# A dense layer with GELU, forward and backward: the first 256 rows of x loaded plainly and turned by TensorE, with changes of order in the first steps, a load moved to another queue, and a last copy made whole

## The chip, the cores and the metric

The kernel runs on one core of a Trainium2 chip. Times are device microseconds of that core, from runs of the whole program. Before the change three runs gave a median of 267.5 us (267.42 to 267.94). A core has five engines with queues of their own: PE (TensorE, matrix products; its weight loads are PEld), DVE (VectorE), ACT (ScalarE), POOL (GpSimd) and SP (SyncE, here only for issuing transfers). Each engine runs its instructions in program order and waits on semaphores for the others.

## The reference, cut to what matters

```python
B, S, D, F = 1, 2048, 448, 1792          # all bf16

def _fwd_reference(x, w1, b1, w2, b2):
    h = jnp.einsum("bsd,df->bsf", x, w1) + b1
    h = jax.nn.gelu(h, approximate=True)
    return jnp.einsum("bsf,fd->bsd", h, w2) + b2

def reference(x, w1, b1, w2, b2, grad_out):
    out, vjp = jax.vjp(_fwd_reference, x, w1, b1, w2, b2)
    return (out, *vjp(grad_out))          # out, gx, gw1, gb1, gw2, gb2
```

With u = x w1 + b1 and h = gelu(u) this is: the output h w2 + b2; q = grad_out w2^T; gh = q times the slope of gelu at u; gx = gh w1^T; gw1 = x^T gh; gw2 = h^T grad_out; and the two bias gradients as sums over the rows of gh and grad_out.

## The kernel before, in words

The 2048 rows are four blocks of 512 (`NB`), the 1792 columns of w1 fourteen tiles of 128, taken in seven pairs a block (`NPAIR`), which makes 28 pairs. For a pair, PE computes u transposed into PSUM (`pu`: three full tiles of 128 of x's 448 columns, and a tail of 64), ACT or DVE copy it out with the bias (`copy_u`, L339 and L341), ACT makes its square, its gelu (`hT`) and a tanh, DVE the slope; PE computes q transposed (`pq`), and DVE multiplies the two into `ghT` (L397). The products of `hT` with w2 and of `ghT` with w1 transposed ("units", tiles `ps`) are PE work that is laid between the pairs' own: each unit is a bank of 128 rows by 448 columns, summed over 14 tiles in two row halves of 64, lower and upper; `side_by_side` issues the halves of two banks alternately. Where one bank is taken up with the other half, `half_product` (L253) puts a wait of PE for its own last product there.

The first 12 pairs are done one by one, with pair f = i + 2 being started in step i; the other 16 are done two by two. All of that order is written out by hand. In single step i PE takes: the first tile of u of pair f (`side_by_side(u_of(f, 0, True), ...)`), a piece of unit work `between[0]`, the second tile of u, `between[1]`, the tails, and so on. In step 1 `between[0]` is the second pair's two tiles for the two units of `uns[1]`. In the loop of double steps, `ahead` (L658) says how many of the three parts of the next pair's first tile come ahead of two units' lower halves; the rest comes between these and the upper halves, 3 in the first double step and 1 later.

At the start, all inputs are fetched by an ordered list of transfers. SP's list begins with x's first block, transposed by the transfer itself in two halves of 256 rows (L146, L149; `wide` reads 512 columns from each row, so that the tail tile's lower 64 rows hold what follows the row, against zero rows in `wt1`), then w1's columns 768 to 1024, a part of w2, grad_out's first block transposed (`load_g(0)`), w2 transposed in parts, and so on. ACT's list has w1's columns 256 to 512 and their rest (the 64 last rows of w1, `load_rest`), the load of its function table with a first activation, then w1's columns 512 to 768 and the rest of 512 to 1024. POOL clears `b1_rows` and fetches b1 into it; DVE turns that in 32 by 32 blocks (L186, L187). PE runs `NWAKE` products of ones (L184) into a bank that nobody reads, and then pair 0 (`pe_u_fulls(0)`, L238, in two halves of 256 rows, for each of the two tiles three products) and its tails (`pe_tail_zeros`, L499).

After the pairs come the weight gradients: gw1 and gw2 by products over all 2048 rows (L768, L779, L800), with the bias sums by DVE (`emit_sum`) and POOL's all-reduce over the partitions (L748, L759) beside them. `gw2_tile` makes the last one in two halves; the second half's bank is copied out by ACT and DVE, half each (L804, L806), and stored by a transfer from ACT's queue. The last lines make SP wait for the last transfers and copies.

The functions that the diff touches:

Of the kernel before, what the change touches and what calls it, by code (L numbers as in the profile page):

```python
# [10 lines left out]
ALU = mybir.AluOpType  # L11
BF16 = mybir.dt.bfloat16
# [7 lines left out]
def kernel(  # L20
# [16 lines left out]
    P = 128  # L37
# [11 lines left out]
    NSTEP = NB * NPAIR  # L49
    NSINGLE = 12  # L50
    LEAD = 2
    NWAKE = 11
    STG = 5
    ROW0 = [SB, 2 * SB, 3 * SB, 0]
    WIDE = (0, 1)
# [82 lines left out]

    AZ = tmp.tile([P, 12, SB], BF16, name="AZ", tag="AZ", bufs=1)
    ones = nc.const_aps.tensor(1.0, [P, SB], BF16)  # L140
    nc.vector.memset(wt1[DL:P, 256:768], 0.0)
    nc.gpsimd.memset(b1_rows[:], 0.0)
    nc.gpsimd.dma_start(out=b1_rows[0:NF, :], in_=b1.rearrange("(ft p) -> ft p", p=P))
    xT[0] = blk.tile([P, KF + 1, SB], BF16, name="xT", tag="xT")
    halves = [slice(0, SB // 2), slice(SB // 2, SB)]
    nc.sync.dma_start_transpose(out=xT[0][:, :, halves[0]], in_=wide(x2, ROW0[0], SB // 2, 0))  # L146
    load_w1(nc.scalar, 256, 512)
    load_rest(nc.scalar, 256, 512)
    nc.sync.dma_start_transpose(out=xT[0][:, :, halves[1]], in_=wide(x2, ROW0[0] + SB // 2, SB // 2, 0))  # L149
    warm = stg.tile([P, 1], F32, name="warm", tag="warm", bufs=1)  # L150
    behind(nc.scalar, nc.scalar.activation(out=warm[:], in_=ones[:, 0:1], func=ACT.Gelu_apprx_tanh))
    load_w1(nc.scalar, 512, 768)
    load_rest(nc.scalar, 512, 1024)
    load_w1(nc.sync, 768, 1024)
    load_w2(nc.sync, 2, 4)
    load_g(0)
# [18 lines left out]
    load_rest(nc.gpsimd, 0, 256)  # L175
    nc.gpsimd.tensor_copy(out=w2T[DL:P, 0, 0:16], in_=w2_first[0:DL, :])
    load_w2T(0, 256)
    for t0, t1 in ((0, 8), (8, NF)):
        nc.sync.dma_start_transpose(out=w1T_sb[:, t0:t1, :], in_=w1[:, t0 * P:t1 * P])
    load_g(1)  # L180

    pw = two_banks(1, "pw")
    for w in range(NWAKE):
        nc.tensor.matmul(pw[:, 0, :], lhsT=ones[:, 0:P], rhs=ones, start=True, stop=True)  # L184
    for c in range(P // 32):
        nc.vector.transpose(b1_t16[c * 32:(c + 1) * 32, :], b1_rows[:, c * 32:(c + 1) * 32])  # L186
    nc.vector.tensor_copy(out=b1T[:], in_=b1_t16[:, 0:NF])  # L187
# [44 lines left out]
    def pe_u_fulls(f):  # L232
        b, p = divmod(f, NPAIR)
        open_u(f)
        for rs in halves if f == 0 else [slice(0, SB)]:
            for a in range(2):
                for kt in range(KF):
                    nc.tensor.matmul(PU[f][a][:, rs], lhsT=w1_f[:, kt, cols(p, a)], rhs=xT[b][:, kt, rs],  # L238
                                     start=(kt == 0 and rs.start == 0), stop=False, skip_group_check=True)

# [309 lines left out]
    for i in range(1, NSINGLE):  # L550
        f = i + LEAD
        if i < 6:
            between = [(uns[1], False, tiles(i)), (uns[0], True, tiles(i)[:1]), (uns[0], True, tiles(i)[1:]), (uns[1], True, tiles(i))]
        elif i == 6:
            between = [(uns[0], True, tiles(i)), (uns[1], False, tiles(i)[:1]), (uns[1], False, tiles(i)[1:]), (uns[1], True, tiles(i))]
        else:
            if i == 7:
                ahead, later = xs, two_units((2, 3))
                slots = [(ahead, False, t) for t in range(6, NF)] + [(later, False, t) for t in range(NF)]
                slots += [(ahead, True, t) for t in range(NPAIR)] + [(later, True, t) for t in range(NF)]  # L560
                slots += [(ahead, True, t) for t in range(NPAIR, NF)]
            between = [slots[2 * c:2 * c + 2] for c in range(5)]
            del slots[0:10]
        open_u(f)
        open_q(i)
        side_by_side(u_of(f, 0, True), u_of(f, 1, True))
        fill(between[0])
        side_by_side(u_of(f, 1), u_of(f, 0))
        fill(between[1])
        pe_tail_pair(f, i, 1)  # L570
        pe_tail_pair(f, i, 0)
        fill(between[2])
        side_by_side(q_of(i, 0), q_of(i, 1))
        fill(between[3])
        side_by_side(q_of(i, 1, True), q_of(i, 0, True))
        if i < 6:
            units_side(uns[0], False, tiles(i + 1))
        elif i > 6:
            fill(between[4])
        if i > 1:  # L580
            act_tanh([i])
        if i == 6:
            evictions(2)
        copy_u(f, "aa")
        if i == NSINGLE - 1:
            evictions(2)
        act_square([f])
        if i == NSINGLE - 1:
            evictions()
        act_gelu([f])  # L590
        if i == 1:
            dve_chain("both 1", "cubic 2", "gate 1", "cubic*u 2", "slope 2", "gh 1", "slope*h 2", "cubic 3")
        elif i < NSINGLE - 1:
            dve_chain(f"both {i}", f"cubic*u {i + 1}", f"gate {i}", f"slope {i + 1}", f"gh {i}", f"slope*h {i + 1}", f"cubic {f}")
        else:
            dve_chain(f"both {i}", f"cubic*u {i + 1}", f"gate {i}", f"slope {i + 1}", f"slope*h {i + 1}", f"gh {i}",
                      f"cubic {f}", f"cubic*u {f}", f"slope {f}", f"slope*h {f}")
        if i == 6:
            evictions()
            open_two(1, 2)  # L600
            xs = open_units[-2:]
            units_side(xs, False, range(0, 6))
        if i == 9:
            nc.gpsimd.dma_start(out=g_low[0:DL, :], in_=gT[1][DL:P, 0, :])
            g_swap[1] = g_low
        if i < 8 or i % 2:
            traffic(i if i < 8 else (i + 7) // 2)
        if i >= 6:
            stores(1 if i > 7 and i % 2 else 2, f - 1)
# [23 lines left out]
    for n in range(nq):  # L633
        i = 10 + n
        k = NSINGLE + 2 * n
        ks = [k, k + 1]
        fs = [k + 2, k + 3] if k + 2 < NSTEP else []
        nxt = [k + 4, k + 5] if k + 4 < NSTEP else []
        if n == 0:
            evictions()  # L640
        act_tanh(ks)
        if n > 0:
            dve_gate(ks, evictions)
        if n == 0:
            pe_u_rows(fs)
        if fs:
            pe_tails(fs if n == 0 else fs[::-1], ks[::-1])
        for f in fs[::-1]:
            copy_u(f, "aa")
        pe_q_rows(ks, nxt)  # L650
        if n == 0:
            a_ = part_a(ks)
            nc.vector.tensor_scalar(out=a_, in0=a_, scalar1=1.0, scalar2=math.sqrt(0.5), op0=ALU.add, op1=ALU.mult)
            dve_chain(f"tanh {k + 1}", f"gate {k + 1}", f"tanh {k}", f"gh {k + 1}", f"gate {k}", f"gh {k}")
        else:
            for q in ks[::-1]:
                dve_gh(q)
        ahead = 1 if n else KF  # L658
        if nxt:
            open_u(nxt[0])  # L660
            side_by_side(u_of(nxt[0], 0, True), u_of(nxt[0], 1, True), slice(0, ahead))
            open_two(1, 2)
            uns = open_units[-2:]
            units_side(uns, False)
            side_by_side(u_of(nxt[0], 0, True), u_of(nxt[0], 1, True), slice(ahead, None))
            units_side(uns, True)
            side_by_side(u_of(nxt[1], 1), u_of(nxt[1], 0))
            side_by_side(u_of(nxt[0], 1), u_of(nxt[0], 0))
        elif fs:
            uns, held = two_units(order_a[2:4]), two_units(order_a[0:2])  # L670
            units_side(uns, False)
            units_side(held, False)
            pe_tails([], [k + 2, k + 3])
            units_side(uns, True)
        if fs:
            act_square(fs)
            act_gelu(fs)
            dve_cubic(fs)
        if i == 15:
            nc.gpsimd.dma_start(out=g_low[DL:P, :], in_=gT[3][0:DL, 0, :])  # L680
            g_swap[3] = g_low
        traffic(i)
        stores(3, k + 1)
# [45 lines left out]
    def f_at(slot):  # L729
        return (2 * FP[slot // 2] + slot % 2) * P  # L730

    sums = []
    for st_ in range(1, NS):
        sums.append(("g", st_))
# [3 lines left out]
    def emit_sum(n):  # L738
        for _ in range(n):
# [10 lines left out]
            else:  # L750
                v = acc[:].rearrange("p (ft f) -> p ft f", f=P)
                b, j = PLACE[st_]
                in0 = gh_nat[:, PLACE[0][0], :, PLACE[0][1], :] if st_ == 1 else v
                nc.vector.tensor_tensor(out=v, in0=in0, in1=gh_nat[:, b, :, j, :], op=ALU.add)  # L754
                if st_ == NS - 1:
                    gb1_w = blk.tile([P, F], BF16, name="gb1_w", tag="ghT")
                    for c in range(4):
# [37 lines left out]
    def gw2_tile(ft, halves):  # L795
        w = D // halves
        for h in range(halves):
            ps = bank_v()
            for st_ in range(NS):
                nc.tensor.matmul(ps[:, 0:w], lhsT=h_nat[ft][:, st_, :], rhs=g_nat[:, st_, h * w:(h + 1) * w],  # L800
                                 start=(st_ == 0), stop=(st_ == NS - 1))
            o = stg.tile([P, SB], BF16, name="st", tag="st")
            c = w // 2 if h == 1 else w
            done = [nc.scalar.copy(out=o[:, 0:c], in_=ps[:, 0:c])]  # L804
            if c < w:
                done.append(nc.vector.tensor_copy(out=o[:, c:w], in_=ps[:, c:w]))  # L806
            queued.append(nc.scalar.dma_start(out=out_4[ft * P:(ft + 1) * P, h * w:(h + 1) * w], in_=o[:, 0:w]))
        return done

# [10 lines left out]
            load_h(ft + 4)  # L820
        emit_sum(3)

    for what in pooled[-8:] + queued[-9:-1] + last:
        behind(nc.sync, what)


# [28 lines left out]
```

## Time and profile before

| | us |
|---|---|
| median of 3 runs | 267.5 |
| the profiled execution, whole | 267.85 |
| its span, first to last instruction | 266.1 |
| first wake-up product of PE starts | 0.77 |
| first product of pair 0 starts | 5.58 |
| PE's wait for the third pair's copies ends | 15.56 |
| first all-reduce of POOL starts | 187.86 |
| last copy's store is issued | 263.60 |

All rows of the profile come from that one profiled execution, on the clock of its span. A row of the timeline gives start, length, engine, line, operation, output and input, count, and in brackets how long the engine stood idle before it and what ended that. The lengths of products are modelled with their pipeline, so the distance between starts says more than a length. "xN" after a row are N instructions merged.

### The profile page before, as it was taken

Reading aid. Unit: us, or ns where it says so; the run is one execution under the profiler, and the core shown is the slowest. Engines: PE = TensorE matmul, PEld = TensorE weight load, DVE = VectorE, ACT = ScalarE, POOL = GpSimd, SP = SyncE. Lnnn points to the kernel's source line nnn. Section 1 sums busy time; section 2 is a strip of 40 time slices with the busy share of each in tenths; the row PEclk is TensorE's granted clock in tenths of the full one; section 3 lists DMA queues with packets and bytes.
Section 4 is the critical chain, followed back from the end, with each engine's and each line's share of the span. In section 5 each row is a group of like instructions: output and inputs, shape, how many; then the busy total and the mean of one; then the engine's idle time right before and its main releaser. Section 6 shows DMA issues by size and latency. Waiting matters only on the chain.

```text
span 266.1 us, 5210 instructions
## 1 busy us (share of the span) xinstructions
PE 261.9 (98%) x2171; PEld 167.8 (63%) x2171; DVE 175.3 (66%) x218; ACT 137.4 (52%) x164; POOL 41.5 (16%) x52
## 2 busy tenths in 40 slices
PE   8999999999999999999999999999999999999995
PEld 3456668888866565555658888864444765555554
DVE  1599999999998978769897731129999990000000
ACT  2799997887997686878759410022111111121111
POOL 1001002400302021010301120220700008900000
PEclk9999999999999999999999999999999999999999
DMA  7999999999999997364381359999311102999841
GB/s 174 243 264 187 171 225 174 286 242 188 233 204 234 211 257 178 41 172 90 115 160 44 72 121 299 352 159 281 90 40 39 49 22 55 218 216 222 203 122 35
DMA packets 111735, 44.47 MB, mean 167 GB/s; under 512 B 91040, under 2 KB 110576, under 8 KB 111712
## 3 DMA queue, kind: packets, MB, share of 16 engines
q1 hardware_dynamic: 104608, 36.14, 64.5%
q0 software_dynamic: 1856, 4.30, 6.6%
q10 hardware_dynamic: 5248, 3.71, 4.6%
q8 instruction: 17, 0.28, 0.4%
q14 instruction: 6, 0.05, 0.1%
HBM read 7.23 MB, written 14.23 MB: 81 GB/s over the span
## 4 chain that ended last, share of the span: by engine, by line
PE 95%; ACT 2%; DMA 1%; DVE 0%; issue 0%; ACTq 0%
PE ps L259 31%; PE ps_v L800 15%; PE pq L259 15%; PE pu L259 14%; PE ps_w L768 14%; PE ps_w L779 2%; PE pw L184 2%; ACT AZ L348 1%; PE pu L238 1%; ACT hT L345 1%; ACT U L339 1%; DMA out_dram<-st 1%; DVE U L341 0%; PE pu L499 0%; ACT AZ L357 0%
## 5 line engine op out<-in xcount | busy, mean ns | idle before, releaser
L259 PE MATMUL pq<-gT,w2T 64*128 64x512 bf16 x386 | 57.5, 376 | 0.0
L259 PE MATMUL ps<-w_sb,hT 64*128 64x448 bf16 x440 | 53.1, 349 | 0.1
L259 PE MATMUL ps<-w1T_sb,ghT 64*128 64x448 bf16 x448 | 51.2, 349 | 0.0
L259 PE MATMUL pu<-xT,w_f 64*128 64x512 bf16 x300 | 43.7, 376 | 0.2 <-ACT U L339 0.2
L339 ACT ACTIVATE U<-pu,b1T 128x512 bf16<-128x512 f32 x54 | 33.5, 690 | 19.3 <-PE pu L259 14.8
L800 PE MATMUL ps_v<-g_nat,h_nat 128*128 128x448 bf16 (+1 forms) x240 | 42.6, 340 | 0.0
L397 DVE SCALAR_TENSOR_TENSOR ghT<-AZ,pq 128x1024 bf16<-128x1024 bf16 x28 | 33.9, 1218 | 12.6 <-PE pq L259 12.0
L438 POOL DMA_DIRECT2D out_dram<-st x32 | 19.9, 626 | 135.8 <-DVE st L437 72.9
L259 PEld LDWEIGHTS <-ghT 64*128 64x128 bf16 x448 | 34.2, 94 | 10.0
L259 PEld LDWEIGHTS <-hT 64*128 64x128 bf16 x440 | 30.0, 94 | 14.6 <-PE ps L259 0.5
L259 PEld LDWEIGHTS <-w2T 64*128 64x128 bf16 x392 | 30.8, 94 | 10.5 <-PE pq L259 0.3
L768 PE MATMUL ps_w<-gh_nat,x_nat 128*128 128x512 bf16 (+1 forms) x192 | 36.5, 352 | 0.0
L800 PEld LDWEIGHTS <-h_nat 128*128 128x128 bf16 x240 | 23.3, 98 | 19.3 <-DMA out_dram<-st 0.3
L357 ACT ACTIVATE AZ<-AZ 128x1024 bf16<-128x1024 bf16 (+1 forms) x20 | 27.8, 1392 | 6.8 <-DVE AZ L353 6.8
L754 DVE TENSOR_TENSOR acc<-acc,gh_nat 128x1792 f32<-128x1792 f32 x14 | 30.0, 2142 | 0.5
L768 PEld LDWEIGHTS <-x_nat 128*128 128x128 bf16 x192 | 18.7, 98 | 17.9 <-issue 0.4
L806 DVE CAST st<-ps_v 128x112 bf16<-128x112 f32 x1 | 0.3, 275 | 43.1 <-DMA out_dram<-st 43.1
L348 ACT ACTIVATE AZ<-U 128x1024 bf16<-128x1024 bf16 (+1 forms) x21 | 28.2, 1342 | 0.9 <-DVE U L341 0.4
L345 ACT ACTIVATE hT<-U 128x1024 bf16<-128x1024 bf16 (+1 forms) x22 | 28.0, 1277 | 0.0
L259 PEld LDWEIGHTS <-w_f 64*128 64x128 bf16 x300 | 21.3, 94 | 10.3 <-issue 0.9
L804 ACT CAST st<-ps_v 128x448 bf16<-128x448 f32 (+2 forms) x15 | 7.5, 501 | 34.8 <-PE ps_v L800 34.8
L435 ACT CAST st<-ps 128x448 bf16<-128x448 f32 x16 | 7.8, 539 | 29.5 <-PE ps L259 27.6
(57 smaller groups left out, 197.0 us busy)
## 6 DMA issues: line engine op xcount, KB each, us to landing
hT_dram<-hT SPq DMA_DIRECT2D x28, 256.0 KB, 3.0
out_dram<-st POOLq DMA_DIRECT2D x32, 112.0 KB, 4.8
x_nat<-in_x_dram SPq DMA_DIRECT2D x1, 1792.0 KB, 10.4
g_nat<-in_grad_out_dram SPq DMA_DIRECT2D x1, 1792.0 KB, 15.7
out_dram<-st ACTq DMA_DIRECT2D x13, 112.0 KB, 3.3
out_dram<-st ACTq DMA_DIRECT2D x9, 128.0 KB, 1.7
w_f<-in_w_dram SPq DMA_DIRECT2D x5, 192.0 KB, 4.2
w_sb<-in_w_dram SPq DMA_DIRECT2D x4, 224.0 KB, 4.0
```

What stands on the lines that cost most here:

```text
L259: mm = nc.tensor.matmul(ps, lhsT=w, rhs=m, start=start, stop=stop, tile_position=(hf.start, 0), skip_group_check=True)
L339: nc.scalar.activation(out=dst, in_=PU[f][a][:], func=ACT.Identity, bias=bias)
L345: nc.scalar.activation(out=rows(hT, r), in_=part_u(r), func=ACT.Gelu_apprx_tanh)
L348: nc.scalar.activation(out=part_a(ks), in_=part_u(ks), func=ACT.Square, scale=math.sqrt(3.0 * GELU_A * GELU_C))
L357: nc.scalar.activation(out=z, in_=z, func=ACT.Tanh, scale=-1.0 / 3.0)
L397: nc.vector.scalar_tensor_tensor(out=rows(ghT, [k]), in0=part_z([k]), scalar=1.0, in1=PQ[k][:], op0=ALU.subtract if single else ALU.add, o ...
L435: nc.scalar.copy(out=st[:, 0:D], in_=self.ps)
L438: pooled.append(nc.gpsimd.dma_start(out=(out2 if self.kind == "o" else gx2)[r:r + P, :], in_=st[:, 0:D]))
L754: nc.vector.tensor_tensor(out=v, in0=in0, in1=gh_nat[:, b, :, j, :], op=ALU.add)
L768: nc.tensor.matmul(ps[:, 0:n * P], lhsT=x_nat[:, st_, kt * P:(kt + 1) * P], rhs=gh_nat[:, b, ft0:ft0 + n, j, :], start=(st_ == 0), stop=(s ...
L800: nc.tensor.matmul(ps[:, 0:w], lhsT=h_nat[ft][:, st_, :], rhs=g_nat[:, st_, h * w:(h + 1) * w], start=(st_ == 0), stop=(st_ == NS - 1))
L804: done = [nc.scalar.copy(out=o[:, 0:c], in_=ps[:, 0:c])]
```

## The change

Ten places change. At the start, rows 512 to 767 of x (the first half of the first block) are loaded untransposed into a corner of the scratch tile `AZ`, two rows on each partition; PE turns them by eight products with an identity of 128 by 128, which POOL makes, into four banks; ACT and DVE copy these into `xT[0]`. DVE clears the tail tile's lower rows of that half. There are 7 wake-up products in place of 11. w1's columns 512 to 768 are fetched by SP behind x's second half, not by ACT. The second part of w1 transposed is fetched after grad_out's second block. In `pe_u_fulls` the order of the six products of a half becomes kt outside, tile inside. In step 1 `between[0]` comes ahead of the first tile of u, and `between[1]` behind it. In the first double step `ahead` is 2. The last half of gw2 is copied by ACT alone, and SP's last waits name the last sum of DVE and that copy.

```diff
-    NWAKE = 11
+    NWAKE = 7
...
+    x_rows = AZ[:, 10:12, :].rearrange("p a s -> p (a s)")[:, 0:2 * D].rearrange("p (j d) -> p j d", j=2)
+    ident = const.tile([P, P], BF16, name="ident")
...
-    nc.sync.dma_start_transpose(out=xT[0][:, :, halves[0]], in_=wide(x2, ROW0[0], SB // 2, 0))
+    nc.sync.dma_start(out=x_rows, in_=x2[ROW0[0]:ROW0[0] + SB // 2, :].rearrange("(p j) d -> p j d", j=2))
+    nc.vector.memset(xT[0][DL:P, KF, halves[0]], 0.0)
+    make_identity(nc, ident[:])
...
-    load_w1(nc.scalar, 512, 768)
     load_rest(nc.scalar, 512, 1024)
+    load_w1(nc.sync, 512, 768)
     load_w1(nc.sync, 768, 1024)
...
-    for t0, t1 in ((0, 8), (8, NF)):
-        nc.sync.dma_start_transpose(out=w1T_sb[:, t0:t1, :], in_=w1[:, t0 * P:t1 * P])
+    nc.sync.dma_start_transpose(out=w1T_sb[:, 0:8, :], in_=w1[:, 0:8 * P])
     load_g(1)
+    nc.sync.dma_start_transpose(out=w1T_sb[:, 8:NF, :], in_=w1[:, 8 * P:F])
...
+    xb = two_banks(0, "xb")
+    xb = [xb[:, 0, halves[0]], xb[:, 1, halves[0]], one_bank(2, "xb")[:, halves[0]], one_bank(3, "xb")[:, halves[0]]]
+    for kt in range(KF + 1):
+        m = P if kt < KF else DL
+        for j in range(2):
+            nc.tensor.matmul(xb[kt][0:m, j::2], lhsT=x_rows[:, j, kt * P:kt * P + m], rhs=ident[:], start=(j == 0), stop=(j == 1),
+                             skip_group_check=True)
+        if kt % 2:
+            nc.vector.tensor_copy(out=xT[0][0:m, kt, halves[0]], in_=xb[kt][0:m, :])
+        else:
+            nc.scalar.copy(out=xT[0][0:m, kt, halves[0]], in_=xb[kt][0:m, :])
...
-            for a in range(2):
-                for kt in range(KF):
+            for kt in range(KF):
+                for a in range(2):
...
+        if i == 1:
+            fill(between[0])
         side_by_side(u_of(f, 0, True), u_of(f, 1, True))
-        fill(between[0])
+        if i > 1:
+            fill(between[0])
+        else:
+            fill(between[1])
         side_by_side(u_of(f, 1), u_of(f, 0))
-        fill(between[1])
+        if i > 1:
+            fill(between[1])
...
-        ahead = 1 if n else KF
+        ahead = 1 if n else 2
...
-            c = w // 2 if h == 1 else w
-            done = [nc.scalar.copy(out=o[:, 0:c], in_=ps[:, 0:c])]
-            if c < w:
-                done.append(nc.vector.tensor_copy(out=o[:, c:w], in_=ps[:, c:w]))
+            done = nc.scalar.copy(out=o[:, 0:w], in_=ps[:, 0:w])
...
-    for what in pooled[-8:] + queued[-9:-1] + last:
+    for what in pooled[-8:] + queued[-9:-1] + [last_sum[0], last]:
```

`make_identity` is a helper of the library, here cut to its two instructions, both of POOL:

```python
def make_identity(nc, identity):                     # masks.py
    nc.gpsimd.memset(identity, 0.0)                  # line 197
    nc.gpsimd.affine_select(out=identity, in_=identity, compare_op=not_equal, fill=1.0,
                            base=0, pattern=[[-1, 128]], channel_multiplier=1)   # line 199
```

The list of the changed program's instructions has one more on POOL between these two, which the source does not write: a reload of POOL's library, with index 0. The same instruction with index 1 stands ahead of the first all-reduce in both programs.

More of the change, by code (lines that the diff above doesn't have):

```diff
@@ L730, in f_at @@
         return (2 * FP[slot // 2] + slot % 2) * P
+    last_sum = []
     sums = []
@@ L753, in emit_sum @@
                 in0 = gh_nat[:, PLACE[0][0], :, PLACE[0][1], :] if st_ == 1 else v
-                nc.vector.tensor_tensor(out=v, in0=in0, in1=gh_nat[:, b, :, j, :], op=ALU.add)
+                last_sum[:] = [nc.vector.tensor_tensor(out=v, in0=in0, in1=gh_nat[:, b, :, j, :], op=ALU.add)]
                 if st_ == NS - 1:
```

## The prediction

> **What bounds the kernel now.** I read the busy shares first, then the chain of waits over the whole span, then the same chain for the first 16 us, then the rows of the engines that the change touches.
>
> ```profile
> span 266.1 us, 5210 instructions
> PE 261.9 (98%) x2171; PEld 167.8 (63%) x2171; DVE 175.3 (66%) x218; ACT 137.4 (52%) x164; POOL 41.5 (16%) x52
> ...
> PE 95%; ACT 2%; DMA 1%; DVE 0%; issue 0%; ACTq 0%
> ```
>
> TensorE is the bound almost everywhere, so what can be gained lies where the chain leaves it: the 2% of ACT. The chain of the first 16 us (start, length, what) shows where:
>
> ```profile
> 0.77 4.85 PE pw L184 x11
> 5.62 2.00 PE pu L238 x12
> 7.62 0.45 PE pu L499 x2
> ...
> 8.09 0.76 DVE U L341
> ...
> 8.93 1.06 ACT AZ L348
> ...
> 14.35 1.17 ACT U L339 x2
> 15.52 0.04 issue
> 15.56 0.59 PE pu L259 x3
> ```
>
> Until 5.6 us PE runs wake-up products; then block 0's first pair; from 8.1 to 15.5 us DVE and ACT carry the chain, and PE waits for the copies of the third pair. From 15.56 on it is PE without a break. So a shift of the first pair's end passes through to the end of the kernel, and PE work put ahead of the wait at 14.98 to 15.56 is won. The rows of PE around the first pair give its pace: eleven 512-column products start 0.427 us apart (4.85 us with the drain), while six of them at 7.89 take 1.29 us to the next (9.18 - 7.89), 0.215 each. The windows give a granted clock of 1.00 for both stretches, but the pace says half rate until about 6.8 us, 6.0 us after the first product.
>
> ```profile
> 7.89 1.46 PE L238 MATMUL pu<-xT,w_f 128*128 128x512 bf16 x6
> 9.18 0.59 PE L499 MATMUL pu<-xT,wt 128*128 128x512 bf16 x2
> ```
>
> POOL at the start, and at its only library reload (line, instruction, count: shortest/median/longest ns, first and last start):
>
> ```profile
> 0.73 0.20 POOL L142 MEMSET b_rows<- 32x128 bf16 x1 [0.29 <-POOLq L839]
> 1.29 0.66 POOL L143 DMA_DIRECT2D b_rows<-in_b_dram  x1 [0.37 <-POOL b_rows L142]
> ...
> 23.41 0.45 POOL L176 COPY w2T<-w_first 64x16 bf16<-64x16 bf16 x1
> ```
>
> ```profile
> L748 POOLq MODIFY_POOL_CONFIG  x2: 37/37/37, 181.7 to 181.8; - x2
> L748 POOL PARTITION_ALL_REDUCE gb_w<-accg x1: 4577/4577/4577, 187.9 to 187.9; - x1
> ```
>
> Two configuration rows of 37 ns end at 181.81; the first all-reduce starts at 187.86. The profile names DVE as what ended that wait (the last sum ends at 187.76), so those 6.05 us may or may not hide a load. The all-reduce itself is not clean: 4.58 us for 448 columns, where the later four take 3.24 to 3.31 us for 512 and 1.87 for 256, which makes about 2.93 for 448. So 1.65 us of the first call are unexplained.
>
> **Part by part. The identity.** `make_identity` is a POOL memset and a POOL affine select, and the changed program's listing has between them a reload of POOL's library, the same instruction that stands before the first all-reduce, which loads another one. POOL is free at 1.95 (1.29 + 0.66). The memset has the 128 elements per partition of L142: 0.20. Two configuration rows: 0.07. That is 2.22. The reload's own cost is bounded by its one row: from 0 (all hidden waiting) to 6.05 + 1.65 = 7.7 us. I take 6.05: an unhidden rest of 1.65 us on the first call speaks for a load that is long against it and was just about done when DVE released POOL. The affine select lies between L142's 0.20 and half of the 256-column all-reduce, 0.93; I take the 0.45 of L176's COPY. The identity is there at 2.22 + 6.05 + 0.45 = 8.7 us; bounds 2.4 and 10.9.
>
> [...]
>
> **The plain load and the turning products.** x's rows (224 KB, SP) take between the 2.6 us of the fastest load of w_f and the 4.0 us of its median: they land at 3.3 to 4.7, ahead of the identity. Seven wake-up products end at 0.77 + 7 x 0.427 = 3.76, and PE then stands until 8.75, so it starts again at half rate (as it did from rest at 0.77). Eight 128-column products: 0.107 each by columns (0.427 / 4), 0.14 by the mean weight load of L184; I take 1.0 together, till 9.75. The copies of 256 columns lie between 0.25 (112 columns) and 0.69 (512) on ACT, 0.28 and 0.75 on DVE: about 0.38 and 0.45, the first done at 8.75 + 0.45 + 0.38 = 9.6, the others ahead of the products that use them, because kt is now the outer loop. First pu product at about 9.8, against 5.58. Twelve at 0.213 make 2.56, two tails at 0.427: the second starts at 12.8 (7.67 before), and DVE's copy follows at 13.45 (0.62 after it at half rate, 0.42 before). 13.45 - 8.09 = 5.36 us late. DVE's two copies and the small memset lie in its 4.2 us wait for b1's rows, ACT's two in its 4.6 us wait for pu: nothing; b1's load and transposes (done at 6.4) stay ahead of it. No row of POOL's later queue is reached: its next one waits until 22.75.
>
> **DMA order.** SP gives up a transpose issue of 1.34 us for a plain one of about 0.5, and takes w1's second part (0.58) from ACT: x's second half is issued at 1.2 rather than 2.13, w1's parts at 2.6 and 3.1 (3.33 and 3.47 before), gT at 4.3 (4.62), everything behind it 0.3 earlier. All of it lands well ahead of a PE that is late. The second half of w1T moves behind gT of block 1: its issue at 34.7 goes to about 37.5, and 6.3 us to landing, as before, makes 43.8. The x units reach its tiles at 44.07 (before: 41.0 against 44.07, and gT 43.0 against 45.57). In a kernel that is 5 us late this costs nothing; without that cover it is 0.3 us from a wait.
>
> **The order in step 1.** PE's wait:
>
> ```profile
> 14.98 0.37 PE L259 MATMUL pu<-xT,w_f 64*128 64x512 bf16 x1
> ...
> 15.56 0.80 PE L259 MATMUL pu<-xT,w_f 64*128 64x512 bf16 x5 [0.20 <-ACT U L339]
> ```
>
> `between[0]`, two pairs at 0.189, moves ahead of it: 0.38 won, if its operand is there (it is what PE used at 14.40). In the late kernel PE arrives with 0.8 us less lead, because its pace is half until 6.0 us after 8.75; ACT's chain, 5.36 late, ends at 20.9, PE's work at 20.1 to 20.9, so the 0.38 is kept to between half and all; I take 0.3.
>
> **`ahead` 2 and the last copy.** At the first double step PE's weight loads wait for its own unit; the last eviction waits twice:
>
> ```profile
> 78.32 1.06 PEld L259 LDWEIGHTS <-hT 64*128 64x128 bf16 x14 [0.50 <-PE ps L259]
> ```
>
> ```profile
> 263.01 0.25 ACT L804 CAST st<-ps_v 128x112 bf16<-128x112 f32 x1 [1.19 <-PE ps_v L800]
> 263.30 0.28 DVE L806 CAST st<-ps_v 128x112 bf16<-128x112 f32 x1 [43.13 <-DMA out_dram<-st]
> 263.60 0.34 ACTq L807 DMA_DIRECT2D out_dram<-st  x1
> ```
>
> PE's starts there are 0.41 apart in place of 0.16 to 0.19; one pair between covers 0.2 (0 to 0.25). The two casts run one after the other; a single one of 224 columns takes 0.35 (the tile before), issue at 263.39: 0.21 won. SP's wait for the last sum instead of DVE's cast costs nothing: that sum is long done.
>
> **Sum.** +5.36 - 0.3 - 0.2 - 0.21 = +4.65. The profiled execution took 267.85 (span 266.1 and 1.75 around it), 0.35 above the median of 267.5; so 267.85 + 4.65 = 272.5 there, and **272.1** for the median. With the reload from 4.2 to 7.7 us and the affine select at its ends: 270.3 to 274.2.
>
> **Rivals.** *The reload is short* (the other side). If the load hides nothing but 1.65 us of a first call, or nothing, the identity is there at 2.7 to 4.3; this decides below a reload of about 2.5 us. For it: the rows show only 37 ns twice, and DVE alone explains the gap. Against: the 1.65 us. Then the products start at about 4.0, the first pu at 5.05; six at 0.213 till 6.33, two more at half rate, four at 0.11: the second tail starts at 7.42 rather than 7.67, 0.25 won, and 0.38 + 0.2 + 0.21 with it: 267.5 - 1.04 = 266.5 (266.1 to 266.9, the upper end with a wait for w1T).
> *Short reload, but PE stays slow.* PE's row now has breaks at 3.76 and around 5; if the 6.0 us that it took to reach full rate count anew from 4.0, full rate comes at 10.0. pu(0) ends 0.57 later, PE is 1.3 late at 9.6 and 0.83 late at 15.56 with the moved pairs; less 0.38 and 0.41: 267.5.
> *A reload in between* (2.5 to 4.2 us): 268 to 270.2.
>
> **Chances.** Forecast 0.68, in between 0.06, short 0.20, short but slow 0.06. A change under 0.2% (0.5 us) can't be told from none here. Faster 0.20, same 0.06, slower 0.74. The likeliest case has 270.3 to 274.2 for itself; to leave out no more than 2 in 10 the range goes down into the short case: 266.4 to 274.2.
>
> **What would show it.** Right: POOL's affine select starts near 8.3, the first xb product stands waiting for POOL from 3.8 to about 8.8, pu products at half pace till 12 or later, and the wait of about 5 us reappears in the chain before the first DVE copy. Wrong: the affine select ends before 4.5; then xb follows the landing of x's rows, and the sign is the other one. The 0.3 shows in a shorter wait of pu for ACT at step 1, the 0.2 in an unbroken row of unit products at the first double step, the 0.21 in the distance from the last cast to the last store's issue.

## The result and the profile after

The changed kernel takes **275.8 us** (median of 4 runs, 275.2 to 276.3), the kernel before, on the same chip, 267.5 (4 runs, 267.4 to 267.9): 1.029 times as long, interval 1.027 to 1.032, or 8.35 us in the medians. The profiled execution is the fastest of the four, 275.23 (span 273.5), while the one of before, 267.85, lay 0.4 above its median; so the two traces show 7.38 of the 8.35 us. Ratios and their intervals, here and below, are reckoned from the fast runs alone (a few runs took over 1.5% longer than the fastest of their kernel), so they need not be the quotients of the medians.

The head of the page after, and the shares of its chain of waits:

```profile
span 273.5 us, 5226 instructions
PE 263.2 (96%) x2175; PEld 148.9 (54%) x2175; DVE 175.7 (64%) x220; ACT 138.2 (51%) x166; POOL 41.3 (15%) x54
...
PE 95%; issue 3%; POOL 0%; ACT 0%; POOLq 0%
```

PE's busy time is 1.3 us longer, the span 7.4. The chain now has 3% that no engine worked on ("issue"), about 8 us, where before ACT had 2%. The chain of the first microseconds (start, length, what) shows where that lies:

```profile
1.94 0.22 POOL ident masks.py:197
2.17 0.07 POOLq masks.py:199 x2
2.23 7.44 issue
9.68 0.29 POOL ident masks.py:199
...
10.01 0.60 PE xb L194 x2
...
11.06 1.58 PE xb L194 x6
12.64 2.67 PE pu L253 x12
```

Between the two configuration rows (L199 of the helper, on POOL's queue) and the affine select lie 7.44 us in which POOL waits for nothing that the profile shows. PE stands behind that and starts the turning products at 10.01; pair 0's first product follows at 12.57 by its own row (the chain has 12.64), where before it was 5.58. Pair 1's first product stands at 15.91, against 7.89: 8.02 late. That is made of three parts, all read from starts of PE's rows: the identity, 10.01 - 5.58 = 4.43; the turning products and the wait inside them, 12.57 - 10.01 = 2.56; and pair 0, 15.91 - 12.57 = 3.34 where it took 2.31, 1.03 more, because it runs at half pace to its end (twelve 256-column products in 2.53 us, 12.57 to 15.10, 0.211 each; the trace's record of the granted clock has full pace from 15.85; before from 6.78). PE's rows of these starts:

```profile
10.01 0.59 PE L194 MATMUL xb<-ident,AZ 128*128 128x128 bf16 x2 [6.10 <-POOL ident masks.py:199]
...
12.57 2.74 PE L253 MATMUL pu<-xT,w_f 128*128 128x256 bf16 x12
...
15.91 1.46 PE L253 MATMUL pu<-xT,w_f 128*128 128x512 bf16 x6
```

Little comes back behind that. Rows of PE in step 1, of its weight loads at the first double step, and of ACT at the end answer to the three that the prediction showed of before:

```profile
23.19 1.19 PE L274 MATMUL pu<-xT,w_f 64*128 64x512 bf16 x6
24.02 0.55 PE L274 MATMUL ps<-w_sb,hT 64*128 64x448 bf16 x2
```

```profile
85.90 2.38 PEld L274 LDWEIGHTS <-hT 64*128 64x128 bf16 x28 [0.31 <-PE ps L274]
```

```profile
270.60 0.35 ACT L825 CAST st<-ps_v 128x224 bf16<-128x224 f32 x1 [1.19 <-PE ps_v L822]
270.98 0.34 ACTq L826 DMA_DIRECT2D out_dram<-st  x1
```

In step 1 six products that take 0.64 without a wait take 0.83 (24.02 - 23.19): 0.19 of waiting is left of the 0.4 before. At the double step a wait of 0.31 is left of 0.50. At the end the cast starts 7.59 later than before and the store's issue 7.38 later. Aligning PE's starts of both traces gives 0.17 won by 20.6 us, 0.05 by 44, 0.23 at the double step and 0.21 at the last copy: 8.02 - 0.66 = 7.36, against 7.38 between the spans.

### The profile page after: what moved, and what is told of

It is laid out like the page before. It is cut to its first block, busy times and chain, and to the rows that moved or that the text cites. A ratio compares the mean times of both kernels' runs of the same rounds, so it can differ in the third digit from the quotient of the medians.

```text
span 273.5 us, 5226 instructions
## 1 busy us (share of the span) xinstructions
PE 263.2 (96%) x2175; PEld 148.9 (54%) x2175; DVE 175.7 (64%) x220; ACT 138.2 (51%) x166; POOL 41.3 (15%) x54
## 4 chain that ended last, share of the span: by engine, by line
PE 95%; issue 3%; POOL 0%; ACT 0%; POOLq 0%
PE ps L274 31%; PE ps_v L822 16%; PE pu L274 15%; PE pq L274 15%; PE ps_w L790 13%; PE ps_w L801 2%; PE pu L253 2%; PE xb L194 1%; PE pu L514 0%; PE ps L440 0%; ACT xT L199 0%; ACT st L825 0%; POOL ident masks.py:199 0%; POOL ident masks.py:197 0%; POOL b_rows L144 0%
## 5 line engine op out<-in xcount | busy, mean ns | idle before, releaser
L274 PE MATMUL pq<-gT,w2T 64*128 64x512 bf16 x386 | 55.5, 376 | 0.0
L274 PE MATMUL ps<-w_sb,hT 64*128 64x448 bf16 x440 | 49.0, 349 | 0.0
L274 PE MATMUL ps<-w1T_sb,ghT 64*128 64x448 bf16 x448 | 48.8, 349 | 0.0
L274 PE MATMUL pu<-xT,w_f 64*128 64x512 bf16 x300 | 41.3, 376 | 0.0
L274 PEld LDWEIGHTS <-ghT 64*128 64x128 bf16 x448 | 28.5, 94 | 15.8
L274 PEld LDWEIGHTS <-hT 64*128 64x128 bf16 x440 | 26.2, 94 | 17.1 <-issue 0.5
L274 PEld LDWEIGHTS <-w2T 64*128 64x128 bf16 x392 | 26.3, 94 | 15.1 <-PE pq L274 1.0
L825 ACT CAST st<-ps_v 128x448 bf16<-128x448 f32 (+1 forms) x15 | 7.6, 508 | 34.8 <-PE ps_v L822 34.8
L274 PEld LDWEIGHTS <-w_f 64*128 64x128 bf16 x300 | 16.1, 94 | 15.0 <-issue 0.7
L793 ACT CAST st<-ps_w 128x512 bf16<-128x512 f32 (+1 forms) x12 | 6.4, 533 | 27.3 <-PE ps_w L790 24.4
```

Source lines behind the costliest of these rows:

```text
L274: mm = nc.tensor.matmul(ps, lhsT=w, rhs=m, start=start, stop=stop, tile_position=(hf.start, 0), skip_group_check=True)
L825: done = nc.scalar.copy(out=o[:, 0:w], in_=ps[:, 0:w])
```

## The experiments

Theory: the reload of POOL's library at the start makes PE late, and nothing behind it takes that up. Rivals: PE's half pace after its stand, the turning products themselves, or the other edits. All were compared with the kernel before on the same chip (267.5, 267.6 and 267.4 us in the three groups). Several of the kernels below spread over 2 to 5 us from run to run.

**The identity without POOL.** DVE makes the row index by doublings, turns it in 32 by 32 blocks and compares, in 2.6 us from 1.31 to 3.88; everything else is as in the changed kernel.

```diff
-    make_identity(nc, ident[:])
+    idx = const.tile([P, P], BF16, name="idx")
+    idx_p = const.tile([P, 32], BF16, name="idx_p")
+    nc.vector.memset(idx[:, 0:1], 0.0)
+    w = 1
+    while w < P:
+        nc.vector.tensor_scalar(out=idx[:, w:2 * w], in0=idx[:, 0:w], scalar1=float(w), scalar2=None, op0=ALU.add)
+        w *= 2
+    for c in range(P // 32):
+        q = slice(c * 32, (c + 1) * 32)
+        nc.vector.transpose(idx_p[q, :], idx[q, q])
+    nc.vector.tensor_tensor(out=ident[:], in0=idx[:], in1=idx_p[:, 0:1].to_broadcast((P, P)), op=ALU.is_equal)
```

> The changed kernel with the identity made by DVE (a column index by seven doublings, turned in 32 by 32 blocks, compared), so that POOL has no library reload at the start. Theory (PE's 6.3 us of standing from 3.7 to 10.0 is the reload and nothing else): the first xb product starts at 3.7 to 4.0, when x's rows have landed; the row of xb products and copies stays 2.56 us long, so the first pu product comes at about 6.4, 0.8 behind before's 5.58; full rate from about 6.8; with the 0.66 us of the other edits 267.1 to 267.6. Rival (the plain load and the turning are slow in themselves): PE still waits, the time stays over 270. Rival (the breaks in PE's row put off its full rate): pu of pair 0 at half pace to the end, 267.8 to 268.5.

267.8 us, ratio 1.000 (0.998 to 1.003). Without the reload the whole 8 us are gone, and the kernel is where it was before the change, 0.2 above the range that was expected. Its rows of PE at the start:

```profile
3.94 0.58 PE L204 MATMUL xb<-ident,AZ 128*128 128x128 bf16 x2
4.98 1.24 PE L204 MATMUL xb<-ident,AZ 128*128 128x128 bf16 x6 [0.46 <-ACT xT L209]
6.15 1.48 PE L263 MATMUL pu<-xT,w_f 128*128 128x256 bf16 x12
```

Turning starts at 3.94 and takes 2.21, and the second tail starts at 7.69 (7.67 before): plain load and turning come out even. The third product, which begins the second bank, waits 0.46 us for ACT's copy of the first: the change cuts both banks out of one tile of two. Later in the same trace PE waits 1.3 us for w1 transposed, which the next but one kernel takes up.

**Two tiles for the two banks**, on top of the last.

```diff
-    xb = two_banks(0, "xb")
-    xb = [xb[:, 0, halves[0]], xb[:, 1, halves[0]], one_bank(2, "xb")[:, halves[0]], one_bank(3, "xb")[:, halves[0]]]
+    xb = [two_banks(0, "xb")[:, 0, halves[0]], two_banks(1, "xb")[:, 0, halves[0]]]
+    xb += [one_bank(2, "xb")[:, halves[0]], one_bank(3, "xb")[:, halves[0]]]
```

> As the run with DVE's identity, and the first two banks of xb are two tiles instead of one. Theory (PE's 0.96 us between the first and the second pair of xb products is a wait for ACT's copy out of the same tile): that wait goes, the row of xb is 0.5 to 0.8 us shorter, the first pu product at about 5.7, 266.8 to 267.2. Rival (the wait is the pipeline's own): no difference from the run before it.

267.9 us, 1.001 (0.998 to 1.004): no difference that these runs can tell, where 266.8 to 267.2 was expected. In the trace the wait is gone: eight products without a break from 3.94 to 5.87, 1.93 us, at half pace throughout. Those of the first three tiles start 0.214 apart, twice the 0.107 that 128 columns make by the 0.427 of 512. But full pace came at 6.72 here and at 5.64 in the kernel without this edit, so the second tail starts at 7.81, no earlier than the 7.69 there.

```profile
3.94 2.00 PE L204 MATMUL xb<-ident,AZ 128*128 128x128 bf16 x8
5.87 1.88 PE L263 MATMUL pu<-xT,w_f 128*128 128x256 bf16 x12
```

**The other edits without the turning**: x's first half by the transposing transfer again, 11 wake-up products, no identity; all else as in the changed kernel.

```diff
-    NWAKE = 7
+    NWAKE = 11
...
-    nc.sync.dma_start(out=x_rows, in_=x2[ROW0[0]:ROW0[0] + SB // 2, :].rearrange("(p j) d -> p j d", j=2))
+    nc.sync.dma_start_transpose(out=xT[0][:, :, halves[0]], in_=wide(x2, ROW0[0], SB // 2, 0))
...
```

> The changed kernel with x's first half transposed by the transfer and 11 wake-up products, as before; all other edits stay (w1's second part by SP, order of step 1, kt outside, ahead 2, order of w1T, last copy). Theory (the x part alone makes the kernel slow, the rest gains): 266.6 to 267.0, with PE's lead growing by 0.2 to 0.4 in step 1, 0.05 at about 44 us, 0.23 at about 78 us, and 0.21 at the end. Rival (the moved load of w1 or the new order costs something at the start): 267.5 or more.

269.1 us, 1.005 (1.002 to 1.008): slower than before, and not the 266.6 to 267.0 expected, although this kernel keeps the edits that win a few tenths. Its PE is 0.41 ahead of before's at 33 us and loses that at the wait for the second half of w1 transposed:

```profile
42.97 0.81 PE L259 MATMUL pu<-xT,w_f 64*128 64x512 bf16 x6
44.89 0.55 PE L259 MATMUL ps<-w1T_sb,ghT 64*128 64x448 bf16 x4 [1.11 <-DMA w1T_sb<-in_w_dram]
```

From the one row to the other are 1.92 us instead of 0.64. So the move of that transfer behind grad_out's second block, which costs nothing in a kernel that is 8 us late, costs here 1.3.

**Neighbouring columns, too**: the second kernel above, with x's rows laid so that each product writes 128 neighbouring columns of the bank, and not every second one.

```diff
-    nc.sync.dma_start(out=x_rows, in_=x2[ROW0[0]:ROW0[0] + SB // 2, :].rearrange("(p j) d -> p j d", j=2))
+    nc.sync.dma_start(out=x_rows, in_=x2[ROW0[0]:ROW0[0] + SB // 2, :].rearrange("(j p) d -> p j d", j=2))
...
-            nc.tensor.matmul(xb[kt][0:m, j::2], lhsT=x_rows[:, j, kt * P:kt * P + m], rhs=ident[:], start=(j == 0), stop=(j == 1),
+            nc.tensor.matmul(xb[kt][0:m, j * P:(j + 1) * P], lhsT=x_rows[:, j, kt * P:kt * P + m], rhs=ident[:], start=(j == 0), stop=(j == 1),
```

> DVE's identity, two tiles, and x's rows laid so that each xb product writes 128 neighbouring columns instead of every second one. Theory (the stride of two makes the products 0.213 apart in place of 0.107): xb's row shrinks by another 0.3 to 0.5 us, first pu product at about 5.3, 266.5 to 266.9, faster than both kernels. Rival (the weight loads set the pace): same as with two tiles alone.

```profile
3.94 1.06 PE L204 MATMUL xb<-ident,AZ 128*128 128x128 bf16 x8
4.93 0.83 PE L263 MATMUL pu<-xT,w_f 128*128 128x256 bf16 x6
6.03 0.81 PE L263 MATMUL pu<-xT,w_f 128*128 128x256 bf16 x6 [0.26 <-DMA xT<-in_x_dram]
```

The eight products now take 0.99 (4.93 - 3.94), at 0.107 from start to start: 0.94 less than with stepped columns. The next thing that PE waits for is x's second half. The time is 268.4, 1.001 (0.998 to 1.004), not the 266.5 to 266.9 expected: the 0.95 us that PE is ahead at 33 us go at the same w1 transfer (from 42.42 to 44.13 are 1.71 us instead of 0.64).

**With w1's second part back ahead of grad_out's second block**: the last kernel, and the one with x's old transfer.

```diff
-    load_g(1)
     nc.sync.dma_start_transpose(out=w1T_sb[:, 8:NF, :], in_=w1[:, 8 * P:F])
+    load_g(1)
```

> DVE's identity, two tiles, neighbouring columns, and the second half of w1T fetched ahead of gT's second block again, as before. Theory (in a kernel that is not late, the later w1T makes PE wait 0.9 to 1.7 us at 43 us): that wait goes, PE's lead over before stays 0.9 to 1.0 us from the start to the end plus 0.23 at 78 us and 0.21 at the end: 266.0 to 266.5, faster than before by 0.4 to 0.5%. Rival (transfers have no room there in either order, so gT is late instead): a wait of pq near 45 us, 267 or more.

> x's first half transposed by the transfer and 11 wake-up products as before, w1T in the old order, the other edits as in the changed kernel. Theory (of the other edits only the w1T order costs): 266.5 to 267.0, some 2 us less than with the new w1T order. Rival (w1's second part by SP delays gT and w2T, and that sets the time): 267.5 or more.

The first takes 267.5 us, 1.000 (0.998 to 1.002), not the 266.0 to 266.5 expected. In its profiled execution PE is 1.33 ahead at 33 us, then waits 0.37 us for grad_out's second block (its next product of q starts at 44.83), the wait that the rival named, and ends 0.97 ahead; but its twelve runs spread from 266.7 to 269.4. The second takes **267.0 us**, 0.998 (0.996 to 0.9995), 2.1 less than the same kernel with the transfer moved, and is the only one whose interval lies below 1, if barely. The profiled executions of the two, 266.94 and 268.24, are 1.30 apart, which is about the wait (1.28 by starts); what makes up the rest of the 2.1 no trace shows. PE at the place of the lost wait:

```profile
42.91 0.81 PE L259 MATMUL pu<-xT,w_f 64*128 64x512 bf16 x6
43.55 0.54 PE L259 MATMUL ps<-w1T_sb,ghT 64*128 64x448 bf16 x4
```

**A reload that nobody waits for.** To the first of these two, POOL's `make_identity` on a tile that nobody reads.

```diff
+    spare = const.tile([P, P], BF16, name="spare")
+    make_identity(nc, spare[:])
```

> As the first kernel of this set, and POOL makes an identity too, in a tile that nobody reads: the reload and the affine select run at the start, no engine waits for them. Theory (the reload costs only who waits for it): POOL's affine select starts at 9.5 to 10.5, the time is that of the first kernel within 0.3. Rival (the load itself holds up transfers or other engines): 0.5 us or more slower.

267.3 us, 1.000 (0.997 to 1.002), as without it. POOL's row:

```profile
10.42 0.63 POOL masks.py:199 TENSOR_SCALAR_AFFINE_SELECT spare<-spare 128x128 bf16<-128x128 bf16 x1 [8.25 <-issue]
```

The load is no shorter than in the changed kernel (8.2 us), and cost nothing by itself here (267.3 against 267.5 without it): the price is PE's wait for it.

**The library already there.** The changed kernel, with one more POOL instruction of library 0 (and a memset for it) behind its last all-reduce, so that this library is the one left when the next execution starts.

```diff
+    spare = const.tile([P, P], BF16, name="spare")
+    nc.gpsimd.memset(spare[:], 0.0)
+    nc.gpsimd.tensor_tensor(out=spare[:], in0=spare[:], in1=spare[:], op=ALU.add)
```

> The changed kernel, with a POOL addition on a spare tile after the last all-reduce, whose library has index 0, so that each execution leaves library 0 in POOL, the one that the next execution's start asks for. Theory A (the reload is paid whatever lies in POOL): affine select at 9.5 or later, 275 to 276.5 as the changed kernel. Theory B (a library that is there already is not fetched again): affine select before 4, PE's xb row from 3.9, 267 to 268.5 from the second execution on.

268.0 us, 1.000 (0.998 to 1.003). The same instruction list at the start, with the same two configuration rows, and no load (start, length, what, and in brackets how long POOL stood before it):

```profile
2.65 0.30 POOL masks.py:199 TENSOR_SCALAR_AFFINE_SELECT ident<-ident 128x128 bf16<-128x128 bf16 x1 [0.27 <-POOL ident masks.py:197]
```

The select starts 0.27 after the memset's end, not 7.5; the configuration rows, at 2.55 and 2.58, end 0.03 before it. The load now lies at the end, between rows at 236.97 and the addition at 244.93, where POOL has nothing else to do. This undoes the load alone, with make_identity, turning and all other edits in place, and gives the same time as DVE's identity.

**What of the loss is not the load.** The changed kernel again, the changed kernel with both repairs of the turning (two tiles, neighbouring columns), and the changed kernel with w1's second part in its old place.

> The changed kernel itself once more, on the chip of the two kernels beside it: 275 to 276.5, the affine select 7.4 to 8.3 us after the configuration rows, first xb product about 0.3 behind it.

> The changed kernel with the reload in its path, and the turning made short: two tiles for the first two banks of xb, neighbouring columns. Theory (of the 2.56 us of xb 1.5 are the wait for ACT's copy and the stride of two): xb's row is 1.0 to 1.2 us, the whole 1.3 to 1.6 us below the changed kernel beside it, 273.8 to 274.6. Rival (PE is at half rate until some 6 us after it starts again, so an earlier start is given back as slower products): 0.5 us or less below it.

> The changed kernel with the second half of w1T ahead of gT's second block again. Theory (in a kernel that is 8 us late the later w1T is covered): within 0.3 us of the changed kernel. Rival (the order of transfers has a share in the 8 us): 0.5 us or more below it.

| kernel | us | ratio | interval |
|---|---|---|---|
| changed | 275.5 | 1.028 | 1.024 to 1.033 |
| with both repairs | 274.1 | 1.023 | 1.018 to 1.027 |
| w1's second part in its old place | 275.1 | 1.027 | 1.022 to 1.031 |

Rows of PE with both repairs:

```profile
10.42 1.15 PE L194 MATMUL xb<-ident,AZ 128*128 128x128 bf16 x8 [6.50 <-POOL ident masks.py:199]
11.50 2.74 PE L253 MATMUL pu<-xT,w_f 128*128 128x256 bf16 x12
```

Turning takes 1.08 where it takes 2.55 in the changed kernel of this group (10.25 to 12.80): 1.47 by the rows, 1.4 by the medians, and no run of the one kernel lies among those of the other. Moving w1's second part back makes 0.4, inside the intervals, and the two traces' spans, 273.1 and 273.2, show none of it.

## Why the prediction was right or wrong

The sign and the mechanism were right: POOL's reload holds the identity back, PE stands behind it and restarts at half pace, and the kernel ends late by almost all of that. The time, 275.8, lies above the 272.1 and above the range's end of 274.2. Two terms of the sum were too small.

- **"The reload's own cost ... I take 6.05."** This failed. The load took 7.44 us in the profiled execution, 7.7 to 7.8 in the three others with the same start, 8.2 where nobody waited for it. The 6.05 came from the row of the first all-reduce before the change, and the traces taken together say that this row held no load. In the seven kernels that ask for no library 0, the one before among them, the first all-reduce starts 0.10 us behind DVE's last sum and is 4.57 to 4.58 long, whether 5.39 or 6.71 us lie between the configuration rows and it. In the six that use library 0 it begins 0.14 to 2.85 us behind that sum, and 6.3 to 8.4 us behind the configuration rows. One row of the first kind (x's old transfer, 5.39 behind the configuration rows) and one of the second (the library resident, 7.37):

```profile
188.46 4.58 POOL L755 PARTITION_ALL_REDUCE gb_w<-accg  x1 [5.53 <-DVE accg L752]
192.70 3.82 POOL L770 PARTITION_ALL_REDUCE gb_w<-accg  x1 [7.44 <-DVE accg L767]
```

Five of the seven, the kernel before among them, start the all-reduce sooner after the rows (5.39 to 6.18 us) than any of the six; and in the run with the library resident a library stayed from one execution to the next (0.03 us behind the same rows, not 7.4). So in the kernel before, library 1 was there already, and DVE alone set the start that I took for the load's end. That is inferred from these rows; no run was made to show it. The bound of 7.7, which I had worked out and not taken, lies near the load by luck, for the 1.65 us in it were no rest of a load: the row is as long with 6.71 us ahead of it as with 5.39. What makes it longer than 2.93 stays open. The rows after the change (line, instruction, count: ns, start) do hold a load:

```profile
L770 POOLq MODIFY_POOL_CONFIG  x2: 37/37/37, 189.7 to 189.7; - x2
L770 POOL PARTITION_ALL_REDUCE gb_w<-accg x1: 3902/3902/3902, 198.2 to 198.2; - x1
```

Here DVE's last sum for it ends at 195.35 (9 additions from 189.45, 5.90 long), 2.8 us before POOL starts, so that DVE doesn't set the start, and the load takes 8.4. In all, the loads here took 7.4 to 8.2 us ahead of the affine select.
- **The affine select, 0.45**: 0.28. The identity was there at 9.97, not 8.7, and the first turning product at 10.01, not 8.75: +1.26.
- **"Eight 128-column products ... I take 1.0 together."** This failed too: 2.56. The 1.0 is what they take in a form that the change does not have (0.99, 1.08). Taking the two banks apart brings 2.56 to 1.93, so 0.63 were a wait of PE for ACT's copy between two banks of one tile, which I had not looked for in the dependences; neighbouring columns bring 1.93 to 0.99, so 0.94 were the stepped columns, `j::2` in the diff, which I priced like plain ones.
- **Pair 0 at half pace, first product to second tail 3.0**: 2.96 (12.57 to 15.53). The size came out with some luck: full pace came 5.84 us behind the first turning product here, near the 6.0 that the prediction took for a fixed time, but 4.2 to 4.8 behind it in the three other traces with the load in PE's way, and in two of these the stretch was 2.5 and 2.6.
- **x's rows land at 3.3 to 4.7**: 3.70. **POOL's later queue and the other transfers**: nothing of them shows in the chain of the first 26 us.
- **0.3 in step 1**: 0.17. **0.2 of `ahead`**: 0.23, though the row was not unbroken, as I had said. **0.21 of the last copy**: 0.21.
- **The move of w1's second part: nothing, "without that cover it is 0.3 us from a wait".** Right in the late kernel; without the cover the wait is there in four of five kernels: 0.9, 1.1 and 1.3 us by PE's rows, and 2.7 in the profiled execution with the library resident, which took 271.7 us. The trace of the fifth, two tiles for the two banks, has none.

The sum with measured terms: 5.36 + 1.26 + 1.51 (2.56 in place of 8.75 to 9.8) = 8.13 late, against 8.02 measured; less 0.66 it is 7.4, the difference of the two traces. The other 1.0 of the medians is where the two profiled executions lie in their runs. Two slips in the prediction's sums are small: 12.8 + 0.62 makes 13.42, not 13.45, and with the affine select at its lower end, 0.20, its case would begin at 270.0, not 270.3.

The rival "the reload is short" came true only where the library was there already, and then the rest was worth nothing, not the 1.0 us that I gave it. The rows show why: the turning was 2.4 long in that trace (3.70 to 6.08), not 1.05, and the w1 wait took the few tenths. The rival "short reload, but PE stays slow" has the time, 267.5, but not by its mechanism: full pace came at 5.6 and 6.7 in the first two kernels with DVE's identity, not at 10.0. What stays open is whether the early lead of the repaired start (1.33 us at 33 us in one trace) can be kept to the end: its median did not move. That lead itself changes with the turn to full pace: 1.33 where it came at 4.5, 0.45 in the kernel with the idle reload, which has the same start on PE, where it came at 6.6.

## What to carry to other kernels

A helper as small as an identity brought a library load of 7.4 to 8.2 us with it here: look in the instruction list for a reload, ask which engine waits behind it, and build the tile on another engine (here 2.6 us on DVE), put the load where POOL is idle, or leave the library resident. When a bound from below and one from above are both to be had from one row, ask what else could have set the start that the lower one rests on, and whether the thing to be sized happened there at all. A transfer that is moved "at no cost" is to be tested in the kernel without the lateness that hides it: here that edit alone decided between 1.005 and 0.998.

## What the runs showed of the hardware

**A library stayed loaded from one execution to the next.** The same two rows of 37 ns stand before a wait of 7.4 us (the changed kernel) or of 0.03 us (the library resident), and only the last library of the execution before differs (that it is this is inferred from the one added instruction at the end, which is all that was changed).

**Stepped columns in PSUM took twice as long here.** Products of 128 columns into every second column started 0.213 apart, into neighbouring ones 0.107, both at half pace; eight took 1.93 and 0.99 us. At full pace it was not measured.

**The time at which PE's pace turned differed from trace to trace.** By the traces' record of the granted clock, which the distances of PE's starts bear out, full pace came at 3.6, 4.1, 4.5, 4.8, 5.6, 5.8, 6.6, 6.7 and 6.8 us in the nine kernels where PE's work goes on without a load to wait for; PE began at about 0.8 in all of them, so the first turn spreads over 3.2 us. The stretches between two turns that the traces show are 3.41 and 6.83 us (second run of the changed kernel, 4.56 to 7.97 to 14.80) and, with the library resident, 40.95 (5.76 to 46.71): 1, 2 and 12 times 3.41, to within 0.03. In the second run of the changed kernel full pace was granted while PE stood and withdrawn before the identity came, and the kernel with both repairs does the same 0.17 us earlier (windows: from:to, length, busy time and count of PE, then of PEld, DVE, ACT and POOL, granted clock, DMA share, GB/s; ahead of a trace's first record, here 4.56, windows say 1.00 whatever the pace):

```profile
4.56:7.97 3.41, 0.00 (x0) 0.00 (x0) 0.00 (x0) 0.00 (x0) 0.00 (x0) 1.00 1.36 243
7.97:14.80 6.83, 4.09 (x18) 2.46 (x18) 1.74 (x7) 0.75 (x2) 0.28 (x1) 0.50 0.93 195
14.80:18.00 3.20, 3.20 (x18) 1.62 (x17) 1.10 (x2) 2.13 (x3) 0.00 (x0) 1.00 1.20 277
```

Half pace came back behind one wait: in the kernel with the resident library, PE stood 2.73 us, until 46.69, for w1 transposed, and the clock was 0.50 for the 3.4 us after it (PE alone):

```profile
46.70:50.10 3.40, 3.40 (x18) 0.50 1.02 193
```

Behind the waits of 0.9 to 1.3 us for the same transfer in three other kernels it did not: four products of 448 columns take 0.38 us there from the first start to the next row (44.89 to 45.27 with x's old transfer), as they do without a wait (43.55 to 43.93).
